# A RetNet recurrence with a SwiGLU block on one core: a written list in place of slots

## The chip, the core and the metric

The kernel runs on one core of a Trainium2 chip. The metric is device time in microseconds (us) from launch to the last result; the times of the kernel before are 250.89, 249.81 and 250.53 us, median 250.53 us. The profile is one further execution, recorded by the hardware profiler.

## What is computed

Two stages, float32 in and out. First a decaying recurrence over 768 positions, for 4 batches and 8 heads of width 64:

```python
state = gamma[h] * state + outer(k[t], v[t])        # 64 x 64 per batch and head
y[t]  = (1 / sqrt(64)) * (q[t] @ state)             # gamma[h] = 1 - 2**(-5-h)
```

Then, on the 3072 rows (batch, position) of 512 = 8 x 64 values each:

```python
xn  = x / sqrt(mean(x*x) + 1e-6) * rms_g
out = (silu(xn @ w_gate) * (xn @ w_val)) @ w_out    # 512 -> 1536 -> 512
```

## The kernel before, in words

The 768 positions are cut into 6 chunks of 128. Within a chunk the recurrence becomes matrix products. With gamma to the power of minus the position folded into v (`vp`) and gamma to the power of the position applied to the result (`ydec`), a chunk's answer is (q k^T, masked to the causal half) times vp, plus q times the state that the earlier chunks left. We write (c, b) for chunk c of batch b.

For each (c, b) there are these pieces. **cast** (L172): q, k to bf16 and v times its decay, on GpSimd for chunks 1 to 5. **t** (L190): q and k are transposed, by TensorE and a copy out of PSUM for chunks 0 and 1, by DMA transposes on SyncE's queue for chunks 2 to 5 (L187). **a** (L208): eight products q k^T of 64 rows, two per pair of heads, into two PSUM banks, and two VectorE multiplications by the causal mask (`am`, L219). **y** (L223): eight products am x vp (L232), for c > 0 four with the state (L237), four products k^T vp for the next state (L244); then VectorE multiplies y by its row decay into SBUF (`x`, L247), ScalarE squares and sums it (L251), GpSimd makes 1/rms of it (`rstd`, L272 and L275), VectorE adds the new products to the state (L259), and GpSimd casts the state to bf16 (L268). **n** and **x** (L280, L290): VectorE multiplies by rstd (and by rms_g from chunk 2 on) to `xn`, which is transposed into `xnT`, by TensorE for chunks 0 and 1 (where rms_g is multiplied in afterwards) and by DMA for chunks 2 to 5.

The SwiGLU block runs a whole chunk, 4 batches x 128 = 512 rows, at a time (`ffn`, L330). For each of 12 slices of the 1536 columns there are four products of 512 columns for g (L335) and four for v (L338), a silu on ScalarE (L340), and a multiplication on VectorE (L341). Then, for each batch, 12 products of 512 columns for the output (L361), a copy on ScalarE (L366) and a store on SyncE's queue. The last batch of the last chunk is computed as two halves of 256 columns (L351).

TensorE does the block of chunk c while the attention of chunk c + 1 is put between its slices: `PLAN` and `PLAN1` say after which slot each piece comes. Chunk 0's attention stands ahead of the whole block, in a list of its own, and the block of chunk 0 begins when all four batches of `xnT` are there. PSUM's 8 banks are two pools of 4, one for attention ("at") and one for the block ("ff"). Each engine runs its instructions strictly in the order in which the program issues them, and a DMA issue is an instruction of the engine that issues it: SyncE issues chunk 0's first batch, all of chunks 1 to 5, the DMA transposes and the stores; GpSimd issues the other loads of chunk 0 (q and k cast on the way) and the weights (cast on the way). The loads of chunk 2 wait until the last part of w_out has landed.

Of the kernel before, what the change touches and what calls it, by code (L numbers as in the profile page):

```python
# [11 lines left out]
AX = mybir.AxisListType  # L12
AF = mybir.ActivationFunctionType
ALU = mybir.AluOpType


@with_exitstack
def kernel(
# [27 lines left out]
    loads = ctx.enter_context(tc.tile_pool(name="loads", bufs=8))  # L46
    work = ctx.enter_context(tc.tile_pool(name="work", bufs=3))
    ffw = ctx.enter_context(tc.tile_pool(name="ffw", bufs=3))
    aps = ctx.enter_context(tc.tile_pool(name="aps", bufs=4, space=bass.MemoryType.PSUM))
    fps = ctx.enter_context(tc.tile_pool(name="fps", bufs=4, space=bass.MemoryType.PSUM))  # L50


    out_v = out.rearrange("(b c p) m -> c b p m", b=B, p=C)

    SYNC_DEP = mybir.DependencyInfo(mybir.DependencyClass.Sync, mybir.DependencyReason.DATA)


    raw = {}

    def load(c, b, after=None):  # L60
        t = []
        for name, src in (("q_f", q), ("k_f", k), ("v_f", v)):
            x = loads.tile([128, H, D], F32, name=name)
            i = nc.sync.dma_start(
                out=x, in_=src[b].rearrange("h (c p) d -> c p h d", p=C)[c])
            if after is not None:
                tc.add_manual_dep(i.ins, after.ins.name, SYNC_DEP, reason="transfer order")
            t.append(x)
        raw[c, b] = t

    raw0 = {}

    def load0(b):
        for name, src in (("qb", q), ("kb", k)):
            x = work.tile([128, DM], BF16, name=name, bufs=6)
            nc.gpsimd.dma_start(
                out=x.rearrange("p (h d) -> p h d", h=H),
                in_=src[b].rearrange("h (c p) d -> c p h d", p=C)[0])  # L80
            raw0[name, b] = x
        x = loads.tile([128, H, D], F32, name="v_f")
        nc.gpsimd.dma_start(out=x, in_=v[b].rearrange("h (c p) d -> c p h d", p=C)[0])
        raw0["v", b] = x

    load(0, 0)
    g_col = const.tile([128, KS], F32, name="g_col")
    with nc.allow_non_contiguous_dma(reason="one column per 128 entries"):
        nc.scalar.dma_start(out=g_col, in_=moe_rms_g.rearrange("(s p) -> p s", p=128))


    pos_i = const.tile([128, NCH], mybir.dt.int32, name="pos_i")
    nc.gpsimd.iota(pos_i, pattern=[[C, NCH]], base=1, channel_multiplier=1)

    lngs = const.tile([128, H], F32, name="lngs")
    for h in range(H):
        nc.vector.memset(lngs[:, h:h + 1], lng[h])
    lnscale = const.tile([128, 1], F32, name="lnscale")
    nc.vector.memset(lnscale, math.log(scale))
    zero = const.tile([128, 1], F32, name="zero")  # L100
    nc.vector.memset(zero, 0.0)
    pos_f = const.tile([128, NCH], F32, name="pos_f")
    nc.vector.tensor_copy(pos_f, pos_i)
    darg = const.tile([128, NCH, H], F32, name="darg")
    nc.vector.tensor_tensor(
# [4 lines left out]
    nc.scalar.activation(vdec, darg, AF.Exp, scale=-1.0, bias=zero)  # L110
    nc.scalar.activation(ydec, darg, AF.Exp, scale=1.0, bias=lnscale)

    warm = const.tile([128, 1], F32, name="warm")
    nc.scalar.activation(warm, zero, AF.Silu)
    mhalf = const.tile([128, 1], F32, name="mhalf")
    nc.vector.memset(mhalf, -0.5)
    ident = const.tile([128, 128], BF16, name="ident")
    make_identity(nc, ident)
    causal = const.tile([128, 128], BF16, name="causal")
    nc.gpsimd.memset(causal, 1.0)  # L120
    nc.gpsimd.affine_select(
        out=causal, in_=causal, compare_op=ALU.is_ge, fill=0.0, base=0,
        pattern=[[1, 128]], channel_multiplier=-1)
    for b in range(1, B):
        load0(b)

    g_bc = const.tile([128, DM], F32, name="g_bc")

    st_f = [const.tile([128, NHP, 2 * D], F32, name=f"st_f{b}") for b in range(B)]
    st_b = [const.tile([128, NHP, 2 * D], BF16, name=f"st_b{b}") for b in range(B)]
    for b in range(B):
        nc.vector.memset(st_b[b], 0.0)


# [3 lines left out]
    wg_v = moe_w_gate.rearrange("(k p) n -> p k n", p=128)  # L140
    wv_v = moe_w_val.rearrange("(k p) n -> p k n", p=128)
    wo_v = moe_w_out.rearrange("(n p) m -> p n m", p=128)
    WB = 384

    landed = {}

    def load_w(i):
        sl = slice(i * WB, (i + 1) * WB)
        nc.gpsimd.dma_start(out=wg_b[:, :, sl], in_=wg_v[:, :, sl])
        landed["w", i] = nc.gpsimd.dma_start(out=wv_b[:, :, sl], in_=wv_v[:, :, sl])  # L150

    def load_wo(i):
        sl = slice(i * 4, (i + 1) * 4)
        landed["wo", i] = nc.gpsimd.dma_start(out=wo_b[:, sl, :], in_=wo_v[:, sl, :])


    cur = {}

    def piece_c(b):
        q_f, k_f, v_f = raw.pop((0, b))  # L160
        for name, x in (("qb", q_f), ("kb", k_f)):
            raw0[name, b] = work.tile([128, DM], BF16, name=name, bufs=6)
            copy = nc.vector.tensor_copy if name == "qb" else nc.scalar.copy
            copy(raw0[name, b], x.rearrange("p h d -> p (h d)"))
        raw0["v", b] = v_f

    def piece_v(b):
        vp = work.tile([128, H, D], BF16, name="vp", bufs=6)
        nc.vector.tensor_tensor(
            out=vp, in0=raw0["v", b], in1=vdec[:, 0, :, None].to_broadcast([128, H, D]), op=ALU.mult)  # L170
        cur[0, b]["vp"] = vp

    def cast(c, b):
        q_f, k_f, v_f = raw.pop((c, b))
        qb = work.tile([128, DM], BF16, name="qb", bufs=6)
        kb = work.tile([128, DM], BF16, name="kb", bufs=6)
        vp = work.tile([128, H, D], BF16, name="vp", bufs=6)
        nc.gpsimd.tensor_copy(qb, q_f.rearrange("p h d -> p (h d)"))  # L178
        nc.gpsimd.tensor_copy(kb, k_f.rearrange("p h d -> p (h d)"))  # L179
        nc.gpsimd.tensor_tensor(  # L180
            out=vp, in0=v_f, in1=vdec[:, c, :, None].to_broadcast([128, H, D]), op=ALU.mult)
        cur[c, b] = dict(qb=qb, kb=kb, vp=vp)
        if c > 1:
            d = cur[c, b]
            for n in "qk":
                t = work.tile([128, NHP, 128], BF16, name=n + "T", bufs=6)
                nc.sync.dma_start_transpose(out=t, in_=d[n + "b"])  # L187
                d[n + "T"] = t

    def piece_t(c, b):  # L190
        if c > 1:
            return
        if c == 0:
            cur[c, b] = dict(qb=raw0["qb", b], kb=raw0["kb", b])
        d = cur[c, b]
        qk_ps = aps.tile([128, 2, NHP, 128], BF16, name="qk_ps", tag="at")
        for i, n in enumerate(("qb", "kb")):
            for hp in range(NHP):
                nc.tensor.transpose(qk_ps[:, i, hp, :], d[n][:, hp * 128:(hp + 1) * 128], ident)  # L199
        qkT = work.tile([128, 2, NHP, 128], BF16, name="qkT")  # L200
        if c == 0 and b in (0, B - 1):
            nc.scalar.copy(qkT[:, 0], qk_ps[:, 0])
            nc.vector.tensor_copy(qkT[:, 1], qk_ps[:, 1])
        else:
            nc.scalar.copy(qkT, qk_ps)
# [245 lines left out]
```

## Time and profile before

| what | us |
|---|---|
| span of the profiled execution, first to last instruction | 248.7 |
| times without the profiler (three runs) | 250.89, 249.81, 250.53 |
| median less that span | 1.83 |
| first product of the block of chunk 0 starts | 24.38 |
| first product of the block of chunks 1, 2, 3, 4, 5 starts | 65.43, 104.53, 141.29, 178.10, 213.59 |
| last product ends | 244.87 |
| TensorE busy / VectorE / ScalarE / GpSimd | 225.9 / 128.1 / 87.4 / 95.2 |

The profiled execution's own time outside its span is not recorded; the difference to the median stands in for it. A stage below is the time from one block's first product to the next block's first product. The rows give, for a group of instructions, its engine, its line and what ended the idle time before it; "<-DVE am L219" after a time means that the instruction waited that long for line 219's result.

### The profile page before, as it was taken

The numbers are of one execution on the slowest core, as the hardware profiler recorded it, in microseconds if no ns is written. First come the engines' busy times: TensorE is split into PE (matmuls) and PEld (weight loads), VectorE is DVE, ScalarE is ACT, GpSimd is POOL, SyncE is SP. The second block draws the span as 40 slices with busy tenths as digits, with TensorE's granted clock in tenths as the row PEclk, the third lists the DMA queues.
The fourth block names the chain that finished last, engine by engine and source line by source line (L and its number), as shares of the span: only waits on it lengthen the run. The fifth ranks groups of instructions, "written<-read, shape, count | busy, mean of one in ns | idle before, by whom it ended". The sixth has DMA issues, their size and how long they took to land.

```text
span 248.7 us, 4121 instructions
## 1 busy us (share of the span) xinstructions
PE 225.9 (91%) x1495; PEld 114.4 (46%) x1521; DVE 128.1 (51%) x215; ACT 87.4 (35%) x170; POOL 95.2 (38%) x177
## 2 busy tenths in 40 slices
PE   1776999979996989999989999989999999999993
PEld 0553445545433545445544445544444444444443
DVE  4796337676234895036894046894047781134300
ACT  6365334531431242232342322433232422332221
POOL 8978144953850236910246910246900211000000
PEclk9997999999999999999999999999999999999999
DMA  9999999898997699955999356999453114200022
GB/s 140 174 195 203 196 219 221 151 199 167 218 290 109 144 222 189 229 127 87 213 209 175 127 131 98 199 207 209 122 115 66 21 21 129 86 0 0 0 87 86
DMA packets 108213, 35.94 MB, mean 145 GB/s; under 512 B 99040, under 2 KB 104928, under 8 KB 108192
## 3 DMA queue, kind: packets, MB, share of 16 engines
q1 hardware_dynamic: 95232, 29.24, 60.8%
q0 software_dynamic: 12288, 6.29, 19.0%
q8 instruction: 12, 0.20, 0.3%
q10 hardware_dynamic: 672, 0.13, 0.3%
q14 instruction: 9, 0.07, 0.1%
HBM read 28.58 MB, written 6.29 MB: 140 GB/s over the span
## 4 chain that ended last, share of the span: by engine, by line
PE 77%; DVE 10%; DMA 5%; issue 3%; ACT 3%; POOL 0%; SPq 0%; DVEq 0%; ACTq 0%
PE o_ps L361 24%; PE v_ps L338 21%; PE g_ps L335 21%; DVE am L219 4%; PE a_ps L215 3%; PE y_ps L232 2%; DMA v_f<-in_v_dram 2%; DVE x L247 2%; DMA k_f<-in_k_dram 2%; PE kv_ps L244 1%; PE y_ps L237 1%; DMA kT<-kb 1%; DVE xn L283 1%; PE o_ps L351 1%; PE qk_ps L199 1%
## 5 line engine op out<-in xcount | busy, mean ns | idle before, releaser
L341 DVE TENSOR_TENSOR hT<-sg,v_ps 128x512 bf16<-128x512 bf16 x72 | 49.4, 687 | 89.6 <-PE v_ps L338 83.2
L338 PE MATMUL v_ps<-xnT,wv_b 128*128 128x512 bf16 x282 | 73.4, 379 | 0.5
L335 PE MATMUL g_ps<-xnT,wg_b 128*128 128x512 bf16 x276 | 72.9, 380 | 0.4
L340 ACT ACTIVATE sg<-g_ps 128x512 bf16<-128x512 f32 x72 | 42.8, 594 | 63.7 <-PE g_ps L335 62.2
L361 PE MATMUL o_ps<-wo_b,hT 128*128 128x512 bf16 x269 | 60.8, 379 | 1.2 <-DMA wo_b<-in_moe_w_out_dram 0.8
L338 PEld LDWEIGHTS <-wv_b 128*128 128x128 bf16 x288 | 28.2, 98 | 34.0
L335 PEld LDWEIGHTS <-wg_b 128*128 128x128 bf16 x288 | 26.6, 98 | 31.5 <-issue 0.9
L361 PEld LDWEIGHTS <-hT 128*128 128x128 bf16 x276 | 26.6, 98 | 30.9 <-issue 0.8
L272 POOL TENSOR_SCALAR ms<-ssq 128x1 f32<-128x1 f32 x24 | 4.5, 189 | 92.4 <-ACT xsq L251 92.3
L251 ACT ACTIVATE xsq<-x 128x512 f32<-128x512 f32 x24 | 15.1, 630 | 48.7 <-DVE x L247 48.6
L219 DVE TENSOR_TENSOR am<-a_ps,causal 128x512 bf16<-128x512 f32 x48 | 30.8, 682 | 2.4 <-PE a_ps L215 2.4
L366 ACT COPY o_sb<-o_ps 128x512 f32<-128x512 f32 x23 | 13.5, 585 | 36.8 <-PE o_ps L361 30.7
L180 POOL TENSOR_TENSOR vp<-v_f,vdec 128x512 bf16<-128x512 f32 x20 | 20.7, 1037 | 3.4 <-DMA v_f<-in_v_dram 3.4
L268 POOL CAST st_b<-st_f 64x256 bf16<-64x256 f32 x40 | 17.3, 432 | 1.3
L247 DVE TENSOR_TENSOR x<-y_ps,ydec 128x512 f32<-128x512 f32 x24 | 16.4, 685 | 1.4 <-PE y_ps L237 0.8
L232 PE MATMUL y_ps<-vp,am 128*128 128x64 bf16 x192 | 12.0, 200 | 5.4 <-DVE am L219 5.1
L178 POOL CAST qb<-q_f 128x512 bf16<-128x512 f32 x20 | 12.1, 606 | 8.7 <-DMA q_f<-in_q_dram 7.9
L283 DVE SCALAR_TENSOR_TENSOR xn<-x,rstd,g_bc 128x512 bf16<-128x512 f32 x16 | 12.5, 784 | 5.5 <-POOL rstd L275 5.5
L232 PEld LDWEIGHTS <-am 128*128 128x128 bf16 x192 | 9.2, 101 | 13.1 <-DVE am L219 9.7
L275 POOL TENSOR_TENSOR rstd<-ms,mhalf 128x1 f32<-128x1 f32 x24 | 13.2, 552 | 2.0
L179 POOL CAST kb<-k_f 128x512 bf16<-128x512 f32 x20 | 12.2, 609 | 2.6 <-DMA k_f<-in_k_dram 1.7
L259 DVE TENSOR_TENSOR st_f<-st_f,kv_ps 128x512 f32<-128x512 f32 x16 | 10.8, 676 | 0.0
(60 smaller groups left out, 125.5 us busy)
## 6 DMA issues: line engine op xcount, KB each, us to landing
out_dram<-o_sb SPq DMA_DIRECT2D x23, 256.0 KB, 2.2
q_f<-in_q_dram SPq DMA_DIRECT2D x21, 256.0 KB, 4.8
k_f<-in_k_dram SPq DMA_DIRECT2D x21, 256.0 KB, 5.0
v_f<-in_v_dram SPq DMA_DIRECT2D x21, 256.0 KB, 5.1
wg_b<-in_moe_w_gate_dram POOLq DMA_DIRECT2D x4, 384.0 KB, 9.6
wv_b<-in_moe_w_val_dram POOLq DMA_DIRECT2D x4, 384.0 KB, 10.7
wo_b<-in_moe_w_out_dram POOLq DMA_DIRECT2D x3, 512.0 KB, 8.3
v_f<-in_v_dram POOLq DMA_DIRECT2D x3, 256.0 KB, 6.2
```

The costliest lines, as they stand in the source:

```text
L180: nc.gpsimd.tensor_tensor(out=vp, in0=v_f, in1=vdec[:, c, :, None].to_broadcast([128, H, D]), op=ALU.mult)
L219: nc.vector.tensor_tensor(out=am[:, i], in0=a_ps[i], in1=causal[:, None, :].to_broadcast([128, NHP, 128]), op=ALU.mult)
L232: nc.tensor.matmul(y_ps[:, h, :], d["am"][:, i, hp, :], d["vp"][:, h, :], start=first, stop=last, skip_group_check=True)
L247: nc.vector.tensor_tensor(out=x, in0=y_ps, in1=ydec[:, c, :, None].to_broadcast([128, H, D]), op=ALU.mult)
L251: nc.scalar.activation(xsq, x.rearrange("p h d -> p (h d)"), AF.Square, accum_out=ssq)
L268: nc.gpsimd.tensor_copy(st_b[b][r, :, i * 64:i * 64 + 64], st_f[b][r, :, i * 64:i * 64 + 64])
L283: nc.vector.scalar_tensor_tensor(out=xn, in0=x, scalar=d["rstd"], in1=g_bc, op0=ALU.mult, op1=ALU.mult)
L335: nc.tensor.matmul(g_ps, wg_b[:, s, sl], xnT[:, s, :], start=s == 0, stop=s == KS - 1)
L338: nc.tensor.matmul(v_ps, wv_b[:, s, sl], xnT[:, s, :], start=s == 0, stop=s == KS - 1)
L340: nc.scalar.activation(sg, g_ps, AF.Silu)
L341: nc.vector.tensor_tensor(out=hT[:, n, :], in0=sg, in1=v_ps, op=ALU.mult)
L361: nc.tensor.matmul(o_ps, hT[:, n, b * C:(b + 1) * C], wo_b[:, n, :], start=n == 0, stop=n == NFF - 1)
```

## The change

The slots, the plans and the lists are replaced by one list of words, `ORDER`. Each word is one operation with its chunk and batch (or its slices and batches), after "@" the engine and after "/" its PSUM banks; the program issues the words in order, so the list sets every engine's sequence, SyncE's and GpSimd's DMAs included, and which of 8 banks each product uses. What the words do differs from before in these points:

- **Chunk 0's mask** `mask0` holds scale times gamma to the power of the row's position in the causal half and 0 elsewhere, made by eight ScalarE exponentials. Chunk 0 has no multiplication by `ydec`.
- **The row decay** of chunks 2 to 5 goes into q's cast, which becomes a GpSimd multiplication. Only chunk 1 keeps `x`; elsewhere the square and the normalisation read y from PSUM. rms_g is multiplied in `N` for every chunk.
- **q k^T visits** of two batches come together in chunks 2 to 5 (one `A` word with four banks), and back to back for batches 3 and 2 of chunk 1.
- **The block from one batch on**: slices 0 and 1 of chunk 0 run for batches 0, 1 and 2 singly, slices 2 and 3 for the first three, and slices 0 to 3 for batch 3. The remaining slices, and all of the later chunks, take 512 rows.
- 141 products of 128 columns without a purpose (`hot`) fill TensorE's sequence in chunk 0, in place of 5 of 512.
- Chunk 1's q and k are cast by GpSimd-issued DMAs. Weights come in pieces of 2 and 3 slices. The end is three parts of 192, 192 and 128 columns.
- The silu and multiplication of a slice, the 10 or 12 products of an output and its last products need not follow each other; slices come in any order.

```diff
+ORDER = """
+Lk.0.1@P Lq.0.0@S hot.48/0 Lk.0.0@S Lq.0.1@P Lv.0.1@S rms@S Lk.0.2@P Lv.0.0@S Lq.0.2@P Lk.0.3@P Cq.0.0@A
+Lv.0.2@S ident iota Tq.0.0/0 wg.0.2 hot.4/2 Ck.0.0@A Eq.0.0@D Tk.0.1/1 masks Tk.0.0/2 Lq.0.3@P Ek.0.1@D hot.10/0
+Lv.0.3@S Ek.0.0@D wv.0.2 A.0.0/34 hot.14/0 wv.2.4 Tq.0.1/5 hot.10/0 wg.2.4 Eq.0.1@D tab M0.0.0 A.0.1/67 V.0.1@P
...
+XE.0.0@A hot.8/1 V.0.3@P Ek.0.3@A N.0.1 Y.0.2/7 g.0.0.2.0.1/5 S.0.2 Lq.1.1@P K.0.0/1 X.0.1/3 s.0.0.2.0.1
+Tq.0.3/0 R.0.2 U.0.0@A hot.5/2 XE.0.1@D Eq.0.3@D g.0.0.2.1.2/4 Lq.1.0@P N.0.2 A.0.3/62 s.0.0.2.1.2 v.0.0.2.0.1/5
+M0.0.3 wv.9.12 X.0.2/3 K.0.1/1 M1.0.3 v.0.0.2.1.2/0 XE.0.2@A Lk.1.2@P h.0.0.2.0.1 U.0.1@A Y.0.3/7 h.0.0.2.1.2
+v.0.0.2.2.3/4 wv.4.6 S.0.3 g.0.0.2.2.3/6 g.0.3.4.0.3/2 B.0.1 s.0.0.2.2.3 v.0.2.3.0.3/3 h.0.0.2.2.3 s.0.3.4.0.3
+R.0.3 v.0.3.4.0.3/5 B.0.0 causal N.0.3 g.0.2.3.0.3/1 h.0.3.4.0.3 Lk.1.0@P X.0.3/0 Tk.1.1/6 s.0.2.3.0.3 K.0.3/4
...
+d.0.3.4.8 x.1.3 Lq.2.0@S d.0.2.8.12 V.1.2@D Lk.2.0@S S.1.3 Lv.2.0@S Y.1.2/4 R.1.3 o.0.2@A K.1.2/1 x.1.2
+d.0.0.8.12 st.0.2@S U.1.2@D Lq.2.1@S S.1.2 d.0.1.0.4/0 N.1.3 o.0.0@A B.1.2 Lk.2.1@S d.0.3.8.12 R.1.2 X.1.3/7
+st.0.0@S d.0.1.4.8 o.0.3@A Ck.2.0@P N.1.2 XE.1.3@A st.0.3@S Cq.2.0@P K.1.3/5 X.1.2/2 tk.2.0 d.0.1.8.12 U.1.3@D
+XE.1.2@A V.2.0@P v.1.0.1.0.4/4 tq.2.0 o.0.1@A B.1.3 v.1.8.9.0.4/1 Cq.2.1@P st.0.1@S g.1.2.3.0.4/3 Lv.2.1@S
...
+Y.2.2/3 M0.2.3 tq.3.0 v.1.10.11.0.4/2 R.2.1 S.2.2 h.1.9.10.0.4 B.2.2 Y.2.3/7 N.2.1 tk.3.0 d.1.0.0.10/5 S.2.3
+R.2.2 h.1.10.11.0.4 XE.2.1@S Cq.3.1@P N.2.2 XE.2.2@S Ck.3.1@P d.1.3.0.12/0 V.3.0@P tk.3.1 R.2.3 tq.3.1 N.2.3
+d.1.0.10.12 o.1.3@A d.1.1.0.10/1 o.1.0@D XE.2.3@S st.1.0@S st.1.3@S A.3.0/4623 Lv.3.1@S d.1.1.10.12 M1.3.1
+Lq.3.2@S v.2.9.10.0.4/7 o.1.1@A M0.3.0 Lk.3.2@S g.2.10.11.0.4/0 M0.3.1 st.1.1@S M1.3.0 g.2.9.10.0.4/5 Lv.3.2@S
...
+    @op
+    def masks(e, bk):
+        ACT.activation(vdec, darg, AF.Exp, scale=-1.0, bias=zero)
+
+        for h in range(H):
+            ACT.activation(mask0[:, h % 2, h // 2], row_f, AF.Exp, scale=lng[h], bias=lnscale)
+        ACT.activation(ydec, darg, AF.Exp, scale=1.0, bias=lnscale)
...
+        if c == 1 and n == "v":
+            after(i, ("q", 1, b))
+        if c == 2:
+            after(i, ("wo", 8))
...
+    def Cq(e, bk, c, b):
+        u = t[c, b]
+        u["qb"] = ring([128, H, D], BF16, "qb", 6)
+        if c == 0:
+            copy(e, u["qb"], u["qf"])
+        else:
+            e.tensor_tensor(out=u["qb"], in0=u["qf"], in1=ydec[:, c, :, None].to_broadcast([128, H, D]), op=ALU.mult)
...
+        for j in range(len(bk) // 2):
+            u = t[c, b + j]
+            u["a"] = [bank(bk[2 * j + i], [128, NHP, 128], F32, "a_ps") for i in range(2)]
...
+        m = mask0[:, i] if c == 0 else causal[:, None, :].to_broadcast([128, NHP, 128])
+        DVE.tensor_tensor(out=u["am"][:, i], in0=u["a"][i], in1=m, op=ALU.mult)
...
+        DVE.scalar_tensor_tensor(out=u["xn"], in0=flat(u.get("x", u["y"])), scalar=u["rstd"], in1=g_bc,
+                                 op0=ALU.mult, op1=ALU.mult)
...
+    def ffn(w, bk, c, n0, n1, b0, b1):
+        m = (b1 - b0) * C
+        p = done[w, c, n0, b0] = bank(bk[0], [128, GT], F32, w[1] + "_ps")
+        for n in range(n0, n1):
             for s in range(KS):
+                nc.tensor.matmul(p[:, (n - n0) * m:(n - n0 + 1) * m], W[w][0][:, s, n * 128:(n + 1) * 128],
+                                 xnT[c][:, s, b0 * C:b1 * C], start=s == 0, stop=s == KS - 1)
...
+    for w in ORDER.split():
+        w, _, bk = w.partition("/")
+        w, _, en = w.partition("@")
+        f, *a = w.split(".")
+        F[f](ENG.get(en), [int(i) for i in bk], *map(int, a))
```

The words, each followed by chunk and batch: L load of q, k or v, C cast of q or k, V the decayed v, T transposes of q or k on TensorE and E their copy, tq and tk the same as DMA transposes, A the q k^T products, M0 and M1 the two mask multiplications, Y the products for y (and, for c > 0, those with the state), K the products for the state, x the multiplication by `ydec` in chunk 1, S square and sum, R rstd, N normalisation, X and XE its transpose and copy (XE@S is the DMA transpose), U the state's update, B its cast to bf16. g and v are the two halves of the block (chunk, slices from, to, batches from, to), s the silu, h the multiplication, d the output's products (chunk, batch, slices from, to), e those of the last batch in parts, o their copy, st the store; wg, wv and wo load weights.

## The prediction

> **What bounds the kernel now.** First the page's busy times and its slices, to see which engine could end last.
>
> ```profile
> span 248.7 us, 4121 instructions
> PE 225.9 (91%) x1495; PEld 114.4 (46%) x1521; DVE 128.1 (51%) x215; ACT 87.4 (35%) x170; POOL 95.2 (38%) x177
> ...
> PE   1776999979996989999989999989999999999993
> ...
> PEclk9997999999999999999999999999999999999999
> DMA  9999999898997699955999356999453114200022
> ```
>
> TensorE (PE) is busy 91% and nothing else reaches 52%; its slices are full from the fourth on, with dips. So what counts is (1) how long it takes to fill TensorE, (2) the gaps, (3) its work itself. The DMA row stands at 9 for most of the first 60 us (a slice is 6.2 us): the start may be bound by transfers too.
>
> Then the timeline of TensorE. In the last stage, with nothing but the block in it, four products of 512 columns start every 0.863 us, so a chunk's 144 products take 31.08 us. The stages last 41.05, 39.10, 36.76, 36.81, 35.49 and 31.28 us. What an attention visit costs is read where nothing waits:
>
> ```profile
> 116.19 1.03 PE L338 MATMUL v_ps<-xnT,wv_b 128*128 128x512 bf16 x4
> 117.06 0.40 PE L232 MATMUL y_ps<-vp,am 128*128 128x64 bf16 x8
> 117.29 0.39 PE L237 MATMUL y_ps<-st_b,qT 128*128 128x128 bf16 x4
> 117.51 0.39 PE L244 MATMUL kv_ps<-vp,kb 128*128 128x128 bf16 x4
> 117.83 0.40 PE L215 MATMUL a_ps<-qT,kT 64*128 64x128 bf16 x8
> 118.16 1.04 PE L335 MATMUL g_ps<-xnT,wg_b 128*128 128x512 bf16 x4
> ```
>
> From start to start: y 0.23, state 0.22, next state 0.22 plus 0.10 before a, a 0.33; together 1.10 us per batch, 4.40 per chunk (3.52 for chunk 5, which makes no state). Chunk 1 has transposes too (0.45 and 0.22 per batch): 0.45 + 0.43 + 0.71 + 0.22 = 1.81, so 7.24. Subtracting block and attention, the first five stages hold 41.05 - 38.32 = 2.73, 39.10 - 35.48 = 3.62, 1.28, 1.33 and 0.89 us of waiting. The timeline says for what:
>
> ```profile
> 51.20 1.02 PE L361 MATMUL o_ps<-wo_b,hT 128*128 128x512 bf16 x4 [0.79 <-DMA wo_b<-in_moe_w_out_dram]
> ...
> 76.51 0.40 PE L215 MATMUL a_ps<-qT,kT 64*128 64x128 bf16 x8 [2.28 <-DMA kT<-kb]
> ...
> 129.67 0.20 PE L232 MATMUL y_ps<-vp,am 128*128 128x64 bf16 x1 [0.47 <-DVE am L219]
> 130.27 0.38 PE L232 MATMUL y_ps<-vp,am 128*128 128x64 bf16 x7 [0.40 <-DVE am L219]
> ```
>
> Late transfers twice, and at each stage's end the last batch's y, which stands directly behind the last slice while VectorE still masks. Before 24.38 TensorE did little: chunk 0's attention is a chain through VectorE and ScalarE.
>
> **The change, part by part.** All sums are against the span of 248.7 us; what lies around it is 1.83 us to the median, kept unchanged.
>
> *Stages of chunks 1 to 5 (before: 65.43 to 244.87, 179.4 us).* Work: 5 x 31.08 + 0.2 for the split last output = 155.6, attention 3 x 4.40 + 3.52 = 16.7. Pairing: two single visits cost 2 x 0.43; sharing the gaps of 0.10 on either side leaves about 0.65, so 0.2 less for each of 8 pairs, 1.6 us (bounds 0, if a's 0.33 is all work, and 3.4, if a second batch cost nothing; the 0.10 gap is the nearest row, so I take 1.6). That is 170.7 us. Waiting: 7.1 us now. The list puts two to four slices (1.7 to 3.5 us) between `A` and the first `Y`, against VectorE's 0.682 us per mask, so the waits of 0.9 to 1.3 us go. What is late next: four masks and a state addition of 0.676 fill 3.4 us where TensorE has 3.7 us before Y.2.0, and XE.2.3 must land before the block of chunk 2. From Y.2.2 that is R.2.2, three GpSimd operations of chunk 3 (1.04 + 0.61 + 1.04), R.2.3 (0.74), N (0.78), a DMA transpose (3.9 in the median), 9.8 us in all, against 9.9 us of TensorE work. With no slack I leave 0.5 us at each of five such places, 2.5 us (bounds 0, and 7.1 as now). Sum 173.2: 6.2 us saved.
>
> *The start (before: first block product 24.38, second block 65.43).* In the list the last mask of chunk 0 (M1.0.3) opens the way to nearly all of the block. ScalarE casts q and k (k's cast ends at 6.09 now), then vdec 0.34 and eight exponentials of 128 x 128 at 0.29 to 0.38 each (the ScalarE rows of that shape at L300): masks ready at 9.5. That is later than the first mask multiplication now (8.61). VectorE then has eight masks (5.4), two v (1.4), two copies (0.8), three N (2.3) and one XE (0.7), 10.6 us, with some 1 us of waiting: M1.0.3 ends near 21.4 and Y.0.3 at 21.65. By then TensorE has done slices 0 and 1 for two batches (1.73 us worth) in its spare time. Behind it remain 31.08 - 1.73 = 29.35 of the block, 7.24 of chunk 1 and 0.66 of chunk 0: 37.25, the second block at 58.9 without waiting. Products of 128 columns take 0.055 us (four in 0.22 by the transposes' row), a quarter of 0.216, so splitting by batch costs nothing. I add 2.1 of the 2.73 us that this stage waits now: 61.0, 4.4 us saved.
>
> TensorE: Matmul & The Clock Gate in the Trainium skill, section "Back-to-back issue gap", gives about 81 ns for such a product in a sustained stream of loads and products, where the trace has 55. By it the 80 narrow products would cost an estimated 2 us more and the second block would start near 63; the measurement decides for 55.
>
> *Transfers at the start.* The third w_out load goes out at 47.9 (behind GpSimd's casts) and SyncE sees it landed at 56.41. By then 10.1 MB have been written, counted from the sizes of the issues; the new list moves 9.05 MB to that point, since chunk 1's q and k are cast on the way. At the same bytes per us the last weight lands at 50.6, at the same number of packets at 56.4. Behind it the list has 6.6 us of TensorE work to the second block: 57.2 to 63.0. My 61.0 lies inside; the upper end is the next rival's start. Now only chunk 0's rows show a cast load: 128 KB land in 5.8 us, 256 KB uncast in 6.2, so bytes count little there.
>
> *Hidden edits.* q's multiplication on GpSimd costs 1.04 in place of 0.606, 16 times: 6.9 us more on an engine with 15.5 to 19.2 us of work in stages of 35 us and more (without that cover, as in the chain above, 0.43 each). Twenty `x` (0.685) leave VectorE: 13.7 us, but it is idle half of a stage, so no time in itself. N with rms_g is 0.784 where it was 0.568 for eight batches; it is in the chain of the start. Square and N now read PSUM: not in the trace for these operations; ScalarE's silu from PSUM takes 0.594 and the square from SBUF 0.630, so between -0.04 and +0.05 each, taken as 0. y's bank is held for some 2.6 us instead of 0.7; with all 8 banks open to both uses the cost is 0, up to the 0.863 of one slice where a bank comes late. The filling products use time in which TensorE waits; they keep the clock up. Now the same eight q k^T products take 0.54 us at 10.87 and 0.33 at 118, and the page's clock falls to 7 in the fourth slice. A full clock is worth 0.2 us for each step of chunk 0's chain, which I count within the 1 us of waiting.
>
> *The end.* Parts of 192, 192 and 128 columns take 2.6 us as the two halves do (2.63), and the last copy is 0.35 instead of 0.42: 3.8 us behind the last product stay.
>
> Sum: 61.0 + 173.2 + 3.8 = 238.0 us span, plus 1.83: **239.8 us**.
>
> **Rivals.** (1) *Transfers or GpSimd's queue hold the start.* GpSimd issues all weights among R, B and V, and in the changed program each of its DMAs from the ninth on waits for an earlier one to land; R.0.3 stands behind wv.4.6, and w_out behind B.0.2. For it: the DMA row is full. Against: w_out is issued late now as well. Then the second block starts at 63.0 to 66, middle 65, and the time is 243.8. (2) *Tight places wait after all.* If the stages lose the 7.1 us they lose now, with the start at 61: 239.8 + 4.6 = 244.4; with both (1) and (2), 248.4. Speaking for it is the lack of slack at each block's start; against it, that a place of 0.1 us too little costs only what it lacks. (3) *Slower.* One mechanism: GpSimd's strict order at the four starts of blocks 2 to 5, where the previous chunk's R stands behind the next chunk's casts, whose loads come late on SyncE's queue behind DMA transposes. Each us by which such a load is late delays the whole block. Against it: now, with the loads issued in one go, the worst such wait is one of 2.28 us. It decides from 10.7 / 4 = 2.7 us per start; at 3.5 us it gives 239.8 + 14 = 253.8. (4) *Pairing saves nothing*, the gap being paid in any case: 241.4, inside the forecast.
>
> **How the numbers follow.** Forecast, with (4): 0.60. (1) alone or (2) alone: 0.25. Both together, near no change: 0.07. (3): 0.08. Own range of the forecast: 235.5 (no waiting and 3.4 for pairing) to 242.5 (pairing saves nothing, second block at 62). The range reaches over (1), (2) and their joint case, with 1.5 us below for a start bound by neither transfers nor waiting: 234.0 to 248.5. A difference of 0.5% is about what a measurement of this kernel can tell from no change, that is 249.3 to 251.8. Half of the joint case falls into it. Faster 0.60 + 0.25 + 0.03 = 0.88, within 0.04, slower 0.08.
>
> **What would show it.** First product of the second block at 61 (63 to 66 for rival 1, with TensorE waiting for weights or R); M1.0.3 ends near 21.4; 0.65 us for a pair's visit; stages of chunks 1 to 5 between 34 and 36 us; at each block's start at most 0.5 us of waiting for a DMA transpose, more for rivals 2 and 3. The prediction is wrong if the start isn't shortened (second block past 65), or if the list's first `Y` of each chunk waits for its masks as the last one does now.

## The result, and the profile after

The changed kernel takes 241.29 us (median of four runs, 240.47 to 241.87) against 250.71 us of the kernel before (249.81 to 251.27): a ratio of 0.963, 95% interval 0.960 to 0.966. The forecast was 239.8 us. The profiled execution took 240.9 us with a span of 239.2, so 1.7 us lie outside the span.

The page of the changed kernel, the lines that answer to those of before:

```profile
span 239.2 us, 4494 instructions
...
PE 226.2 (95%) x1707; PEld 123.2 (51%) x1733; DVE 119.8 (50%) x207; ACT 85.9 (36%) x174; POOL 105.5 (44%) x177
...
PE   7868989999899999989999999999999999999994
...
PEclk9999999999999999999999999999999999999999
DMA  9999999988989694997828799197786105201004
```

TensorE is as busy as before (226.2 us for 225.9), in a shorter span. Its first four slices read 7, 8, 6 and 8 instead of 1, 7, 7 and 6, but 11.6 us of the busy time are the filling products of chunk 0 (the page's row of L215), which compute nothing. The clock row has lost its 7. The DMA row starts as full as before.

| point in the trace, us | before | predicted | after |
|---|---|---|---|
| first block product | 24.38 | none | 18.71 |
| last `y` of chunk 0 (Y.0.3) starts | 18.73 | 21.65 | 23.62 |
| last transposition of chunk 0 (X.0.3) starts | 22.98 | none | 27.82 |
| block of chunk 1 starts | 65.43 | 61.0 | 63.54 |
| from there to the last product's end | 179.4 | 173.2 | 172.4 |
| behind the last product | 3.8 | 3.8 | 3.2 |

The blocks of chunks 2 to 5 start at 97.17, 135.34, 170.03 and 204.25; the last product ends at 236.0. The 9.5 us of span are thus 1.9 in the start, 7.0 in the five stages and 0.6 at the end. In the stages the work fell by 1.7 (the pairs, below), so the waiting fell from 7.1 to about 1.8 us: 172.4 - (155.6 + 16.7 - 1.7). TensorE's rows name 1.2 us of that 1.8 (0.70, 0.36 and 0.16 us).

TensorE's timeline of the changed kernel, the start (start us, duration us, then the instruction and in brackets what it waited for):

```profile
18.71 0.61 PE L425 MATMUL g_ps<-xnT,wg_b 128*128 128x128 bf16 x8
...
22.71 0.40 PE L387 MATMUL xt_ps<-ident,xn 128*128 128x128 bf16 x4 [0.95 <-DVE xn L374]
...
23.62 0.67 PE L342 MATMUL y_ps<-vp,am 128*128 128x64 bf16 x8
...
28.94 1.06 PE L425 MATMUL v_ps<-xnT,wv_b 128*128 128x128 bf16 x16
29.84 1.03 PE L425 MATMUL g_ps<-xnT,wg_b 128*128 128x512 bf16 x3
...
36.27 0.39 PE L342 MATMUL y_ps<-vp,am 128*128 128x64 bf16 x8 [1.04 <-POOL vp L292]
...
63.54 0.81 PE L425 MATMUL v_ps<-xnT,wv_b 128*128 128x512 bf16 x3
```

The block begins 5.67 us earlier than before, on one batch, though chunk 0's own chain ends 4.8 us later (X.0.3 at 27.82 for 22.98). No product of the start waits for a weight. The 16 narrow products from 28.94 to 29.84 take 0.056 us each, as taken.

The same view, the stages:

```profile
73.13 0.62 PE L324 MATMUL a_ps<-qT,kT 64*128 64x128 bf16 x16
73.68 1.04 PE L425 MATMUL v_ps<-xnT,wv_b 128*128 128x512 bf16 x3
...
87.62 0.40 PE L342 MATMUL y_ps<-vp,am 128*128 128x64 bf16 x8
...
97.17 1.02 PE L425 MATMUL v_ps<-xnT,wv_b 128*128 128x512 bf16 x4 [0.36 <-DMA xnT<-xn]
...
102.35 0.38 PE L402 MATMUL kv_ps<-vp,kb 128*128 128x128 bf16 x4 [0.70 <-POOL vp L292]
```

A pair of batches takes 0.55 us of q k^T, 0.65 with the gap ahead of it; the last `y` of a stage (87.62) waits for no mask; a block's first product waits 0.36 us or nothing. One wait of 0.70 stands at 102.35.

Why Y.0.3 came 2 us late stands in VectorE's timeline of the changed kernel:

```profile
12.46 0.69 DVE L292 TENSOR_TENSOR vp<-vf,vdec 128x512 bf16<-128x512 f32 x1 [0.53 <-DMA vf<-in_v_dram]
...
15.56 0.69 DVE L292 TENSOR_TENSOR vp<-vf,vdec 128x512 bf16<-128x512 f32 x1 [1.21 <-DMA vf<-in_v_dram]
...
21.91 0.75 DVE L374 SCALAR_TENSOR_TENSOR xn<-y_ps,rstd,g_bc 128x512 bf16<-128x512 f32 x1 [1.35 <-POOL rstd L368]
22.58 1.28 DVE L332 TENSOR_TENSOR am<-a_ps,mask 128x512 bf16<-128x512 f32 x2
```

VectorE waits 3.8 us in its chain (these three, and 0.71 for a transposition), where the prediction had 1. Its masks of batch 3 (22.58) stand behind a normalisation that waits for `rstd`. GpSimd's timeline says why that is late:

```profile
19.00 1.04 POOL L292 TENSOR_TENSOR vp<-vf,vdec 128x512 bf16<-128x512 f32 x1 [2.04 <-DMA vf<-in_v_dram]
...
21.05 0.18 POOL L366 TENSOR_SCALAR ms<-ssq 128x1 f32<-128x1 f32 x1
```

GpSimd stands at V.0.3 until batch 3's v has landed, and R.0.2 is behind it. That load took 12.82 us from its issue by SyncE at 6.12 to its landing; of chunk 0's four v loads the median is 9.8, where all of v took 4.6 us over the whole run.

### The profile page after: what moved, and what is told of

Same layout as the page of the kernel before. It is cut to its first block, busy times and chain, and to the rows that moved or that the text cites. A ratio compares the mean times of both kernels' runs of the same rounds, so it can differ in the third digit from the quotient of the medians.

```text
span 239.2 us, 4494 instructions
## 1 busy us (share of the span) xinstructions
PE 226.2 (95%) x1707; PEld 123.2 (51%) x1733; DVE 119.8 (50%) x207; ACT 85.9 (36%) x174; POOL 105.5 (44%) x177
## 3 DMA queue, kind: packets, MB, share of 16 engines
q1 hardware_dynamic: 90176, 27.96, 55.1%
## 4 chain that ended last, share of the span: by engine, by line
PE 77%; DMA 13%; SPq 3%; POOL 2%; issue 1%; DVE 1%; POOLq 0%
PE v_ps L425 23%; PE g_ps L425 23%; PE o_ps L450 22%; DMA vf<-in_v_dram 10%; DMA qb<-in_q_dram 3%; PE y_ps L342 2%; PE a_ps L324 2%; PE y_ps L346 2%; SPq L253 2%; PE kv_ps L402 1%; POOL vp L292 1%; PE o_ps L472 1%; POOL st_b L417 1%; SPq L393 1%; DVE xn L374 0%
## 5 line engine op out<-in xcount | busy, mean ns | idle before, releaser
L443 DVE TENSOR_TENSOR hT<-sg,v_ps 128x512 bf16<-128x512 bf16 (+2 forms) x74 | 49.0, 669 | 69.4 <-PE v_ps L425 37.3
L425 PE MATMUL v_ps<-xnT,wv_b 128*128 128x512 bf16 (+2 forms) x316 | 70.1, 357 | 0.7 <-DMA xnT<-xn 0.4
L425 PE MATMUL g_ps<-xnT,wg_b 128*128 128x512 bf16 (+2 forms) x308 | 68.3, 357 | 0.5
L435 ACT ACTIVATE sg<-g_ps 128x512 bf16<-128x512 f32 (+2 forms) x74 | 43.2, 585 | 67.0 <-PE g_ps L425 56.2
L450 PE MATMUL o_ps<-wo_b,hT 128*128 128x512 bf16 x266 | 62.6, 379 | 0.6 <-issue 0.2
L292 POOL TENSOR_TENSOR vp<-vf,vdec 128x512 bf16<-128x512 f32 x20 | 20.9, 1042 | 20.8 <-DMA vf<-in_v_dram 20.7
L141 ACT COPY o_sb<-o_ps 128x512 f32<-128x512 f32 (+2 forms) x20 | 11.1, 555 | 42.5 <-PE o_ps L450 41.4
L280 POOL TENSOR_TENSOR qb<-qf,ydec 128x512 bf16<-128x512 f32 x16 | 17.1, 1070 | 19.4 <-DMA qf<-in_q_dram 19.3
L374 DVE SCALAR_TENSOR_TENSOR xn<-y_ps,rstd,g_bc 128x512 bf16<-128x512 f32 x20 | 15.0, 748 | 15.0 <-POOL rstd L368 14.3
L360 ACT ACTIVATE xsq<-y_ps 128x512 f32<-128x512 f32 x20 | 11.9, 596 | 20.3 <-PE y_ps L346 18.4
L215 PE MATMUL hot_ps<-one 128*128 128x128 bf16 x141 | 11.6, 242 | 1.1 <-DVE one L148 1.1
## 6 DMA issues: line engine op xcount, KB each, us to landing
wo_b<-in_moe_w_out_dram POOLq DMA_DIRECT2D x3, 512.0 KB, 12.8
```

The lines of the kernel that those rows point to most:

```text
L141: (e.copy if e is ACT else e.tensor_copy)(out, in_)
L280: e.tensor_tensor(out=u["qb"], in0=u["qf"], in1=ydec[:, c, :, None].to_broadcast([128, H, D]), op=ALU.mult)
L292: e.tensor_tensor(out=u["vp"], in0=u["vf"], in1=vdec[:, c, :, None].to_broadcast([128, H, D]), op=ALU.mult)
L374: DVE.scalar_tensor_tensor(out=u["xn"], in0=flat(u.get("x", u["y"])), scalar=u["rstd"], in1=g_bc, op0=ALU.mult, op1=ALU.mult)
L425: nc.tensor.matmul(p[:, (n - n0) * m:(n - n0 + 1) * m], W[w][0][:, s, n * 128:(n + 1) * 128], xnT[c][:, s, b0 * C:b1 * C], start=s == 0, s ...
L435: ACT.activation(sg[:, :cols], done["wg", c, n0, b0][:, :cols], AF.Silu)
```

## The experiments

The theory to test: the gain is the early block, the pairs, and waits that the order removes; what is missing in the start are late loads of v behind which GpSimd and VectorE stand. Rivals are named with each run. All ratios are to the kernel before on the same chip. Line numbers of the runs differ by a few from those above. The change itself, run a second time, gives the size of a difference that means something:

> The change as it is, beside the two improved lists on the same chip: 241.3, within 0.6.

240.38 us (239.06 to 241.04), ratio 0.958, interval 0.955 to 0.961. The second block started at 64.13 (63.54 in the first run) and Y.0.3 at 25.94 (23.62) in its profile. So the same kernel's start varies by 0.6 to 2.3 us, its median by 0.9, which is more than the 0.6 expected, and its single times within this run by 2.0. A difference of about 1 us between two of the runs below shows nothing.

**Pairs split.** The second visit of chunks 2 to 5 comes behind the next product of the list:

```diff
-A.2.0/5237 h.1.5.6.0.4 v.1.3.4.0.4/6 M0.2.1
+A.2.0/52 h.1.5.6.0.4 v.1.3.4.0.4/6 A.2.1/37 M0.2.1
```

> The change with the q k^T visits of two batches taken apart in chunks 2 to 5: the second batch's visit comes one block product group (or one y) later. Nothing else moves. Theory, TensorE's own work sets the stages: a pair's visit takes 0.65 us in the trace and two single ones 0.43 each, so 8 x 0.21 = 1.7 us more, 243.0 us. Rival, the pair only changes where the masks are made and the visit is hidden or its gap is paid anyway: 241.3, within 0.4. A later second mask may add a wait at the places without slack; then over 244, with y waiting for am.

245.22 us, ratio 0.979 (0.974 to 0.985). TensorE's timeline of this run:

```profile
72.93 0.40 PE L327 MATMUL a_ps<-qT,kT 64*128 64x128 bf16 x8
73.26 1.04 PE L428 MATMUL v_ps<-xnT,wv_b 128*128 128x512 bf16 x3
74.23 0.40 PE L327 MATMUL a_ps<-qT,kT 64*128 64x128 bf16 x8
...
75.41 1.02 PE L428 MATMUL g_ps<-xnT,wg_b 128*128 128x512 bf16 x4 [0.45 <-DVE am L335]
...
164.11 0.41 PE L345 MATMUL y_ps<-vp,am 128*128 128x64 bf16 x8 [1.39 <-DVE am L335]
```

A single visit takes 0.33 + 0.10 us, two 0.86, a pair 0.65: 0.21 for each of 8 pairs, 1.7 us. The profiled span is 4.6 us longer than the change's. The rest of that are waits for masks, 0.45, 0.39, 0.45 and 1.39 us, 2.7 together: the second batch's q k^T now ends 1.63 us behind the first one's start (74.56), the pair's 0.55, so its masks come 1.1 us later, and the list has no room for that.

**No filling products** (the 12 `hot` words, 141 products, left out; they are no part of the result).

> The change without its 141 filling products. Theory, they keep the clock up through chunk 0: without them transposes, q k^T and y in chunk 0 take about 0.2 us longer per step of the chain and the narrow first block products run at half rate, so the second block starts 1 to 3 us later, 242.5 to 244.5. Rival, the fill is idle time painted busy and the start is set by VectorE, ScalarE and transfers: 241.3, within 0.5.

240.45 us, ratio 0.961 (0.957 to 0.965): the same. My theory fell. In TensorE's timeline the rows of chunk 0 are slower (eight q k^T products at 9.13 take 0.54 us from start to start, 0.33 in the change), and Y.0.3 starts at 24.30, 0.7 us later. But the second block starts at 62.6, earlier than in the change; the wait of 1.04 us for V.1.1 is gone. The state product of chunk 3 then waits longer than the change's 0.70:

```profile
9.13 0.61 PE L325 MATMUL a_ps<-qT,kT 64*128 64x128 bf16 x8 [0.52 <-DVE kT L142]
...
102.39 0.38 PE L403 MATMUL kv_ps<-vp,kb 128*128 128x128 bf16 x4 [1.76 <-POOL vp L293]
```

The end is the same.

**The block of chunk 0 only with four batches** (the pieces of slices 0 to 3 put together behind X.0.3):

```diff
-g.0.0.2.0.1/5 s.0.0.2.0.1 g.0.0.2.1.2/4 s.0.0.2.1.2 v.0.0.2.0.1/5 v.0.0.2.1.2/0
+g.0.0.1.0.4/5 s.0.0.1.0.4 v.0.0.1.0.4/3 h.0.0.1.0.4 g.0.1.2.0.4/1 s.0.1.2.0.4
...
```

> The change, but the block of chunk 0 starts only when all four batches of xnT are there; slices 0 to 3 then run with 512 rows. Theory, TensorE's work behind chunk 0's chain sets the start: three quarters of slices 0 to 3 (6 groups of 0.863 = 5.2 us) move from before about 28 us to behind it, less 0.7 us of x wait that they cover, so 4 to 5 us more, 245.5 to 246.5. Rival, weights and chunk 1's loads set when the second block starts: under 1.5 us more, 241.3 to 242.8, with the block waiting less for loads later on.

248.49 us, ratio 0.991 (0.988 to 0.994); second block at 70.33, 6.8 later. Its TensorE timeline, and then the busy time of the engines in three stretches (stretch, length, busy of PE, PEld, DVE, ACT, POOL with counts, granted clock, DMA share, GB/s):

```profile
28.05 0.61 PE L388 MATMUL xt_ps<-ident,xn 128*128 128x128 bf16 x4 [3.52 <-DVE xn L375]
...
31.86 1.91 PE L426 MATMUL v_ps<-xnT,wv_b 128*128 128x512 bf16 x4
```

```profile
24.50:28.00 3.50, 0.02 (x1) 0.00 (x0) 0.75 (x1) 0.69 (x2) 3.21 (x8) 0.85 1.80 175
28.00:34.00 6.00, 5.73 (x29) 3.54 (x31) 0.97 (x3) 2.16 (x4) 5.85 (x10) 0.52 1.72 207
34.00:40.00 6.00, 6.00 (x32) 2.76 (x29) 2.63 (x4) 1.88 (x4) 5.06 (x7) 1.00 1.37 201
```

TensorE has nothing to do for 3.52 us, and then works at a granted clock of 0.52 for 6 us, which costs 6.00 x 0.48 = 2.9 us of work. The change does 5.3 us of block work before X.0.3 (six groups of eight narrow products at 0.45 and four of 384 columns at 0.65). 5.3 + 2.9, less the wait of 1.04 for V.1.1, which is gone here, is 7.2, near the 6.8. The theory had 4 to 5 us; the clock was not in it. The block from one batch on thus brings work and keeps the clock. Filling products in this gap might keep the clock too; no run tried that. The Trainium skill, TensorE: Matmul & The Clock Gate, section "What's actually happening", has the clock halve after an idle window of some 3.4 us; these rows agree. A gap that long was not needed, though: in the run with five words, below, TensorE stood 2.06 us, and the granted clock then read 0.50. And without this part the list's second block is later (70.33) than that of the kernel before (65.43): the list's chain of chunk 0 is the slower one, and only with the early block in it does the start get shorter.

**Row decay back to `x`** in chunks 2 to 5 (a plain cast of q, and the 16 multiplications on VectorE; `x` gets six buffers instead of three, here and in the next run):

```diff
-            e.tensor_tensor(out=u["qb"], in0=u["qf"], in1=ydec[:, c, :, None].to_broadcast([128, H, D]), op=ALU.mult)
+            copy(e, u["qb"], u["qf"])
-S.2.0 B.2.0
+x.2.0 S.2.0 B.2.0
...
```

> The change with the row decay of chunks 2 to 5 back behind y: q's cast is a plain cast again, and VectorE multiplies y by the decay before the square. Theory, VectorE's 16 x 0.69 us lie beside TensorE, but the chain from the last y to the next block's first product gets 0.7 us longer at four starts that had at most 0.5 us of slack: 0.5 to 3 us more, 241.8 to 244.3. Rival A, GpSimd's queue was the tight one and gets 0.45 us per cast back: 241.3 or less. Rival B, VectorE's extra work delays masks and the multiplication behind the silu everywhere: over 246.

244.66 us, ratio 0.977 (0.973 to 0.980): 3.4 us worse. TensorE's timeline of this run:

```profile
103.33 0.38 PE L405 MATMUL kv_ps<-vp,kb 128*128 128x128 bf16 x4 [1.76 <-POOL vp L295]
...
128.25 0.38 PE L345 MATMUL y_ps<-vp,am 128*128 128x64 bf16 x7 [0.40 <-DVE am L335]
```

and VectorE's, ahead of that wait at 128.25:

```profile
121.46 0.75 DVE L377 SCALAR_TENSOR_TENSOR xn<-x,rstd,g_bc 128x512 bf16<-128x512 f32 x1 [1.83 <-POOL rstd L371]
...
125.72 2.47 DVE L335 TENSOR_TENSOR am<-a_ps,causal 128x512 bf16<-128x512 f32 x4
128.12 0.67 DVE L413 TENSOR_TENSOR st_f<-st_f,kv_ps 128x512 f32<-128x512 f32 x1
```

The normalisation at 121.46 waits 1.83 us for `rstd`: `x` stands ahead of the square, which here starts 1.58 us behind its y (0.72 in the change). From there VectorE runs almost without a gap, and the four masks of batches 2 and 3 start at 125.72 (123.91 in the change), and `y` waits. Of these 1.81 us, 0.98 were there already at the state product (103.33 for 102.35): the v that it waits for was issued as in the change (97.12 for 97.20) but took 5.1 us to land instead of 4.1, which the edit doesn't explain. VectorE is busy only 53% of the span, but what counts is where. The theory's place, a block's first product, waits only 0.2 to 0.4 us. The waits in TensorE's rows, beyond those of the change, name some 2.6 of the 3.8 us by which the profiled span is longer; where the rest lies I didn't place. So the row decay is worth up to 3.4 us, some 1.0 of it the late load.

**Chunk 0's mask back** (the plain causal mask and `x` in chunk 0):

```diff
-        m = mask0[:, i] if c == 0 else causal[:, None, :].to_broadcast([128, NHP, 128])
+        m = causal[:, None, :].to_broadcast([128, NHP, 128])
-S.0.0
+x.0.0 S.0.0
...
```

> The change with chunk 0's mask as the plain causal half and the row decay multiplied behind y on VectorE, as in chunk 1. Theory, VectorE's chain of chunk 0 sets Y.0.3: four multiplications of 0.69 more, but the first mask can start some 1.5 us earlier because the eight exponentials are gone, so Y.0.3 and the second block come 0.5 to 1.5 us later, 241.8 to 242.8. Rival, the masks' exponentials hold the chain: the start gets shorter by about 1 us, 240.3.

240.87 us, ratio 0.961 (0.956 to 0.967); second block at 63.35. The same as the change: this part is worth nothing that can be measured. The theory, 0.5 to 1.5 us later, fell. The exponentials are not what holds the first mask: it starts at 10.28 (10.66), in both runs behind a copy that waits for a transposition (1.61 us here, 2.01 in the change). Chunk 0's first `y` starts 0.8 us earlier (12.43), since V.0.1 found its v landed and ran at 11.52 (12.46, after a wait of 0.53). By Y.0.3, at 24.71 (23.62), that is gone.

**V.0.3 behind R.0.2 on GpSimd**, the wait that the trace blamed for the late start:

```diff
-XE.0.0@A hot.8/1 V.0.3@P Ek.0.3@A
+XE.0.0@A hot.8/1 Ek.0.3@A
-Tq.0.3/0 R.0.2 U.0.0@A
+Tq.0.3/0 R.0.2 V.0.3@P U.0.0@A
```

> The change with one word moved: on GpSimd, batch 3's decayed v of chunk 0 (V.0.3), which stood waiting for its load till 19.0 us, comes behind the load issue Lq.1.1 and R.0.2. Theory, GpSimd's strict order delayed R.0.2 by 1.4 us and chunk 1's first q load by 3 us, and with them the last mask of chunk 0 and V.1.1: the second block starts 1 to 2 us earlier, 239.3 to 240.3. Rival, TensorE or the transfers behind have no room, or V.0.3 now comes late for Y.0.3: 241.3, within 0.5.

240.81 us, ratio 0.961 (0.956 to 0.966). Y.0.3 starts at 22.91, and the wait of 1.04 for V.1.1 is gone, but the second block starts at 63.39. GpSimd's timeline of this run:

```profile
22.93 0.76 POOL L266 DMA_DIRECT2D wv_b<-in_moe_w_val_dram  x1
23.67 0.90 POOL L255 DMA_DIRECT2D kb<-in_k_dram  x1
...
25.29 0.90 POOL L419 CAST st_b<-st_f 64x256 bf16<-64x256 f32 x2
26.28 0.19 POOL L368 TENSOR_SCALAR ms<-ssq 128x1 f32<-128x1 f32 x1
```

R.0.3 (26.28) stands behind three DMA issues and a state cast. X.0.3 starts at 27.96 as before (27.82), now with a wait of 1.06. One wait gave way to the next on the same queue.

**The kernel before, last `y` one slot later** (nothing else changed):

```diff
-PLAN = dict(..., y=(6, 8, 10, 12), n=(8, 10, 12, 13), x=(8, 10, 12, 14))
+PLAN = dict(..., y=(6, 8, 10, 13), n=(8, 10, 12, 14), x=(8, 10, 12, 15))
```

> The kernel before with one plan changed: in chunks 2 to 5 the last batch's y comes one slot later, behind the first output of the block instead of ahead of it (its n and x one slot later too). Theory, the waits of 0.9 to 1.3 us at each stage's end are y waiting for its two masks: four waits go, 3.5 to 4.5 us less, 246.5 to 247. Rival, the wait moves to the next block's first product, which then waits for the last DMA transpose: 250.5, within 1.

247.89 us, ratio 0.990 (0.984 to 0.996). The waits of `y` for masks at the stages' ends are gone, and one block start pays for it:

```profile
105.12 1.04 PE L335 MATMUL g_ps<-xnT,wg_b 128*128 128x512 bf16 x4 [2.14 <-DMA xnT<-xn]
```

The second block starts 1.2 us later than before (66.60) and the q k^T behind it waits 0.60 us for `kT` instead of 2.28; the moved pieces, all of chunks 2 to 5, are the cause of neither. The time lies between the theory's and the rival's. So some 2 to 3 us of the list's gain were to be had in the old scheme by three numbers; the rest needs `y` and the transpose behind it to move independently.

**The kernel before with the row decay in q's cast** for chunks 2 to 5 (no `x` there):

```diff
-x = work.tile(...); nc.vector.tensor_tensor(out=x, in0=y_ps, in1=ydec[:, c, :, None]..., op=ALU.mult)
+x = y_ps
```

> The kernel before with one part of the change alone: in chunks 2 to 5 the row decay goes into q's cast on GpSimd, and the square and the normalisation read y from PSUM. Theory, at each of the four stage ends VectorE makes xn, x, st_f and then the two masks that TensorE waits for; without x (0.60 from start to start) the masks come 0.6 us earlier: 4 x 0.6 = 2.4 us less, 247.6 to 248.6. Rival, x lies beside TensorE's work in the old order, and y's bank held longer makes q k^T wait instead: 250.2, within 0.8, or more.

251.88 us, ratio 1.004 (1.002 to 1.007): a little slower. My theory fell. TensorE's timeline of this run:

```profile
122.56 0.23 PE L220 MATMUL a_ps<-qT,kT 64*128 64x128 bf16 x1
123.45 0.38 PE L220 MATMUL a_ps<-qT,kT 64*128 64x128 bf16 x7 [0.67 <-DVE xn L291]
```

The stage-end waits are gone, but `y` now holds its bank until the normalisation, and the second product of `a` waits 0.67 us for a bank six times, 4.0 us. With four banks for attention the same edit costs what it saves; with the list's choice of eight it is worth 3.4.

**Four moved words** for the waits of the start (V.0.3 as above, B.0.1 behind R.0.3, B.1.2 behind R.1.2, V.0.2 behind Eq.0.2):

```diff
-... B.0.1 s.0.0.2.2.3 ... R.0.3 v.0.3.4.0.3/5
+... s.0.0.2.2.3 ... R.0.3 B.0.1 v.0.3.4.0.3/5
-... B.1.2 Lk.2.1@S d.0.3.8.12 R.1.2
+... Lk.2.1@S d.0.3.8.12 R.1.2 B.1.2
-... M1.0.1 V.0.2@D Y.0.1/2 ... Eq.0.2@D
+... M1.0.1 Y.0.1/2 ... Eq.0.2@D V.0.2@D
```

> The change with four words moved: V.0.3 behind R.0.2, B.0.1 behind R.0.3 and B.1.2 behind R.1.2 on GpSimd, V.0.2 behind Eq.0.2 on VectorE. Theory, with V.0.3 alone the second block did not come earlier because R.0.3 then waited behind B.0.1 and the last R of chunk 1 behind B.1.2; in every run of the list so far the last transpose of chunk 1 waits 0.65 us for that. That wait goes and up to 1 us at R.0.3: the second block starts at 61.5 to 62.8, 239.3 to 240.5. Rival, loads set the start: the wait turns up at another word, 240.8, within 0.5.

241.24 us, ratio 0.962 (0.958 to 0.965): no gain. The second block starts at 62.32 (63.54), the third at 96.04 (97.17), and then it is given back. From the timeline of all engines in this run:

```profile
95.17 0.83 SPq L465 DMA_DIRECT2D out_dram<-o_sb  x2
...
96.07 0.44 SPq L255 DMA_DIRECT2D vf<-in_v_dram  x1
...
101.18 1.04 POOL L294 TENSOR_TENSOR vp<-vf,vdec 128x512 bf16<-128x512 f32 x1 [9.19 <-DMA vf<-in_v_dram]
102.27 0.38 PE L404 MATMUL kv_ps<-vp,kb 128*128 128x128 bf16 x4 [1.75 <-POOL vp L294]
```

The load of v for batch 1 of chunk 3 stands on SyncE's queue behind DMA transposes (the last issue ends at 94.67) and two stores, and lands 5.1 us later, beside them, at 101.18, as in the change (101.26). It was issued 1.1 us earlier than there (96.07 for 97.20) and took that much longer to land (5.11 for 4.06); why, the runs leave open. So the state product starts at 102.27 (102.35), though the third block came 1.1 us earlier.

**These words, no fill, and that load right behind k's** (`Lk.3.1@S Lv.3.1@S`):

> The same four words, the filling products left out, and the load Lv.3.1 issued by SyncE right behind Lk.3.1 instead of behind two stores. Theory, the 0.70 us that the state products of chunk 3 wait for that v go, and the fill is worth nothing: 0.7 us below the four words alone, 238.7 to 240. Rival, the earlier load collides with the DMA transposes XE.2.1 to XE.2.3 and the third block starts later, or the fill is needed once the chain is shorter: as the four words alone or up to 1 us more.

239.92 us (239.69 to 242.66), ratio 0.959 (0.955 to 0.964); not to be told from the change. The wait for v is gone, but the DMA transposes behind the load are 1.3 us later than with the four words alone (the last one for qT at 93.46 for 92.18), and q k^T of chunk 3 waits for one:

```profile
95.99 0.40 PE L325 MATMUL a_ps<-qT,kT 64*128 64x128 bf16 x8 [2.06 <-DMA qT<-qb]
...
97.25 1.69 PE L426 MATMUL v_ps<-xnT,wv_b 128*128 128x512 bf16 x4 [0.33 <-DMA xnT<-xn]
```

Behind this wait the granted clock reads 0.50 from 98 to 100 us, and four products that take 0.86 us elsewhere take 1.48. This is the profile of one of the two long executions (241.78 and 242.66; the other four took 239.69 to 239.93), and two things were changed at once. So a load placed too early on that queue can cost a wait of its own; whether it does in the usual execution isn't shown.

**The four words, and the load ahead of the two stores only:**

```diff
-XE.2.3@S st.1.0@S st.1.3@S A.3.0/4623 Lv.3.1@S
+XE.2.3@S Lv.3.1@S st.1.0@S st.1.3@S A.3.0/4623
```

> The changed kernel with the four moved words of e8 and the load of v of chunk 3, batch 1 issued ahead of two stores on SyncE's queue. Theory: what gave e8's 1.1 us back was this one load, issued at 96.07 and landed at 101.18 behind the two stores and the DMA transposes. Issued some 0.9 to 1.3 us earlier, with the 4.6 us that such a load takes in the median, it lands near 100, GpSimd's multiplication ends near 101, the wait of 1.75 us before the state product at 102.27 falls to about 0.5, and the gain reaches the end: last product about 1.2 us earlier than in e8, 239.6 to 240.2 us. Rival: the next loads and transposes on the same queue pin the time again (the products after 102 wait for chunk 3's other batches, or the stores held back keep o_sb's buffers): the wait moves, and the time stays at 240.8 or above.

238.21 us (238.01 to 239.3, five runs), ratio 0.9523, interval 0.9495 to 0.9552: faster than the change (0.9599 to 0.9662); the interval of its second run (0.9546 to 0.9613) it just touches. It is also below the expected 239.6 to 240.2. The same view as in the run before:

```profile
93.81 0.58 SPq L253 DMA_DIRECT2D vf<-in_v_dram  x1
...
94.91 0.83 SPq L463 DMA_DIRECT2D out_dram<-o_sb  x2
...
97.06 1.04 POOL L292 TENSOR_TENSOR vp<-vf,vdec 128x512 bf16<-128x512 f32 x1 [5.76 <-DMA vf<-in_v_dram]
...
99.43 0.39 PE L402 MATMUL kv_ps<-vp,kb 128*128 128x128 bf16 x4
```

Measured from the third block's start (95.12 here, 96.04 there), the load goes out 1.3 us earlier, namely right behind the transposes, and lands in 3.25 us instead of 5.11, with the stores now behind it (they go out at 94.91, while it is under way). The state product waits for nothing. The last product ends at 233.1 us, 2.9 earlier than with the four words alone. Only the wait of 1.75 is the moved load's: the third block comes 0.9 earlier because the second did already (61.13 for 62.32), with the same words ahead of both, so that is the start's own variation. This is the best version of the study.

## Why the prediction was right, and where it wasn't

The forecast was 1.5 us under the measured time, and part of that closeness is luck: the start came 2.5 us later than the sum had it, the stages took 0.8 us less and the end 0.6 less, so the errors partly cancelled in the span (239.2 for 238.0).

**Five stages: right.** 172.4 us against 173.2. The work term held (pairs 0.65 by the rows, 1.7 us by the run with split pairs, predicted 1.6), and of the waits 1.8 are left where 2.5 were allowed. The waits at the stages' ends went, as said, since the masks have room; a block's start waits at most 0.36 us for a DMA transpose. The sign "between 34 and 36 us" did not hold for each stage: they last 33.6, 38.2, 34.7, 34.2 and 31.7 us, since the list puts output products of one chunk behind the next block's first ones (12 at 103.44), so only the sum can be compared.

**The start: mis-sized.** The term "10.6 us, with some 1 us of waiting" of VectorE's chain should have been 3.8 us of waiting beside 9.4 of work; the first mask multiplication began 1.2 us late too (10.66 for 9.5), behind a copy that had waited 2.01 for a transposition. (The prediction's 9.5 + 10.6 + 1 is 21.1, not the 21.4 that it went on with.) Y.0.3 started at 23.62 and the second block at 63.54, inside the range that I had given to the first rival. What failed is that I priced the loads of chunk 0 by the rows of before and looked at the weights for what lands last; no weight was waited for. It was v, with 9.8 us in the median, and GpSimd's strict order behind it. The mechanism of the first rival was right in kind (an instruction of GpSimd behind a late DMA) and named the wrong place at first: V.0.3 ahead of R.0.2; R.0.3 behind the weights, which it did name, is the next in line (the run with V.0.3 moved). The terms from Y.0.3 to the second block, 39.35 predicted, took 39.9.

**"No time in itself" for `x`: wrong.** Taking the 16 multiplications of chunks 2 to 5 from VectorE is worth up to 3.4 us in the list, some 1.0 of it a late load that the edit doesn't explain, though VectorE is idle half of the time: the masks, `x` and the block's multiplications fall in the same places. In the total this didn't show, since the sum of the stages took their waits as gone anyway. In the old scheme alone it brings nothing, and there y's held bank is what I had priced at up to a slice: 0.67 us six times.

**Hidden edits.** Square from PSUM 0.596 us (0.628 from SBUF in the same run), N 0.748 (0.784): within the bounds. The Trainium skill, Perfetto Trace Analysis, section "Optimizing Scalar/DVE Operations", gives ScalarE some 93 ns of overhead on SBUF and 51 on PSUM, an estimated 42 ns less; here it is 32. The 0.056 us of a narrow product stand against the 81 ns of TensorE: Matmul & The Clock Gate, section "Back-to-back issue gap": the row of before was the better guide. The mask of chunk 0 and the filling products are worth nothing that the runs can tell. The multiplication by the decay on GpSimd took 1.07 us (1.04).

**The third rival** (a load late behind DMA transposes on SyncE's queue, with GpSimd waiting) exists, once and for 0.70 us, in the stage of chunk 2; it needed 2.7 us at four places, and here it held a state product and not a block's start. In the runs without fill and with four words this place took back a gain of the start, and putting it right took out a wait of 1.75 us.

**What the parts are worth** can't be added up: the early block 7.2 us, the row decay up to 3.4, the pairs 1.7 (3.9 with the masks that they delay), each taken out of the full list, are more than the 9.4 together. Each part needs the order that was written around it. The difference between the start's 1.9 us and the early block's 7.2 is for the most part the list's own slower chunk 0; why that chain is slower, beyond the loads of v, the runs leave open.

## What to carry to other kernels

When a stretch of a list gets shorter and the time stays, look for the next instruction that starts at the same absolute time as before: it may hang on a queue, as here, where the load went ahead of two stores and the wait was gone. That is one case. That an engine is idle half of the time doesn't say that its work is free: read whether it runs without a gap just ahead of a wait. An edit that removes work can be worth nothing or less without the buffers that it then holds longer, so try it in the scheme where it is to live.

## What the runs showed of the hardware that I had not expected

- A load of v (256 KB on SyncE's queue) landed in 4.6 us in the median of the whole run, but in 6.0 to 12.8 in the first 20 us, beside cast loads and weights (the DMA row at 9). A sum that takes the median for such a load puts what waits for it too early.
- 3.5 us without a product were followed by 6 us at a granted clock of 0.52, and 2.06 us without one, in the run with five words, by 2 us at 0.50. In the run without filling products the rows of chunk 0 are slow as well (0.54 us for eight q k^T), while the granted clock of 8 to 15 us reads 1.00: there the rows tell more than the clock's column. The cause is open.
- Two stores ahead of a load cost it twice on SyncE's queue: 1.4 us until it was issued (94.67 to 96.07, though their data had been ready at 93.4) and some part of its landing: 5.11 us in that run, 4.06 in the change with the same two stores ahead of it, 3.25 ahead of them, so 0.8 to 1.9. Why it differs is open.
